# Two 3x3 convolutions with group norms: the order of the rows of the transformed input

## The chip, the cores and the metric

The kernel runs on one core of a Trainium2 chip, as one launch. The metric is the device time of an execution in microseconds; a median over several executions stands for a kernel. TensorE multiplies matrices and accumulates in PSUM; VectorE, ScalarE and GpSimd work element by element on SBUF and PSUM; SyncE issues most DMAs. In the profile they are PE (and PEld for its weight loads), DVE, ACT, POOL and SP.

## What is computed

A residual block on x of 2 images, 512 channels, 64 x 64 pixels, in bf16:

```python
h = conv3(_silu(gn(x, g1, be1)), w1)
emb = _silu(t_emb) @ w_emb
h = h + emb.reshape(B, C, 1, 1)
h = conv3(_silu(gn(h, g2, be2)), w2)
return x + h
```

`gn` normalizes each of four groups of 128 channels over its channels and all pixels, `conv3` is a 3x3 convolution with padding 1 from 512 to 512 channels.

## The kernel before, in words

**Tiling.** Channels lie in four blocks of 128 (`ct` of the input, `ot` of the output), one block on the 128 partitions. An image is cut into two chunks of 32 rows, so there are four chunks in each of the two layers. One chunk and one `ot` make a "set" (`one_set`, L789); 32 sets follow each other.

**Transform.** The convolution is done in a transformed form. Rows go in groups of four output rows (`TH`), eight groups to a chunk (`TR`). For each group six rows of input are combined into six "positions" 0 to 5; for each position the kernel columns `kx` = 0, 1, 2 are three taps, read with an offset of one element each. A chunk of a `ct` has a tile V (eight tiles `Vbuf`, four per chunk, in turn; so a tile is written again for the chunk after next). In it a position takes NI = 8 x 66 = 528 elements, its "slot". The weights are transformed in the same way into tiles U. TensorE multiplies U by V into one of three PSUM buffers `acc` and ScalarE and VectorE combine the positions into output rows y.

**Two kinds of chunk.** In the first chunk of layer 0 all six positions are stored and multiplied (`col` false in `is_col`, L561). In all others positions 0 and 5 are transformed along the columns too and lie behind the four slots of positions 1 to 4, from element 4 NI on; there slots 0 to 3 hold positions 1, 2, 3, 4. In the first chunk slot i holds position i. The last two chunks of layer 1 replace the products of positions 1 and 3 by another form (`v_more`, `v_more_split`, `rhs_more_split`, L540 to L559).

**Who writes V.** `make_v` (L584) is VectorE's work for a block, with some operations on ScalarE (`scaled`). Positions come in pairs: with `pr` and `qs`, two terms each, from vt, one operation writes positions 1 and 3 as their sums (L601) and one writes 2 and 4 as their differences (L602). In the first chunk a third writes 0 and 5 from the activated input `a_tmp` (L604) and a fourth adds `rs` (a src tile) to both (L605). The destination of each is one access with two blocks of 528 elements; `vv` (L593) gives it for the first two.

**Who reads V.** `row_pair` (L671) makes the matmuls of a pair of positions, 3 taps x 4 `ct` each, through `rhs_row` (L564); `col_pair` (L681) reads the parts behind 4 NI. A set uses the pairs (1, 3), then for a `col` chunk columns (1, 2), then (2, 4), then (0, 5) or columns (0, 3).

**Order.** Every operation is first a node with an estimated cost in a planner (`_Plan`, L25). Its dependencies are exact masks of elements (`region`, L62), and the planner lists the operations of each engine in its own order, mixing sets, chunks and the weights' transform (`u_blocks`, L485, which needs transposes on TensorE, L386, and copies on ScalarE, L510). All VectorE operations of a kind have one line (L317 for two tensors, L322 and L330 for others), all main matmuls have L660, and ScalarE's have L347. The planner only orders: the waits (semaphores) between and within engines are put in afterwards by the framework, from what each instruction reads and writes.

Of the kernel before, what the change touches and what calls it, by code (L numbers as in the profile page):

```python
# [187 lines left out]
def kernel(  # L188
# [24 lines left out]
    TR = 8  # L213
# [13 lines left out]
    WARM = (11, 12)  # L227
    DVE_SUMS = (1,)
    COL0 = (1, 2, 3)
    POS_ORDER = (1, 3, 2, 4, 0, 5)  # L230
    assert C % P == 0 and E % P == 0 and C // 4 == P and H % CR == 0 and NFREE == 512

    x_v = x.rearrange("b (ct p) h w -> b ct p (h w)", p=P)
# [304 lines left out]
    more_buf = lambda ct: (a_tmp + src)[ct]  # L538

    def v_more(V, X):  # L540
        rows = lambda kx, st: view(V, kx, [[2 * NI, 2], [WP, TR], [st, W // st]])
        dst = lambda o, n: view(X, o, [[n * TR, 2], [n, TR], [1, n]])
        tt(dst(0, W), rows(0, 1), rows(2, 1), ALU.subtract)
        tt(dst(4 * NC, W // 2), rows(1, 2), rows(2, 2), ALU.add)
        tt(dst(6 * NC, W // 2), rows(2, 2), rows(1, 2), ALU.subtract)
# [3 lines left out]
    def v_more_split(V, at, D):  # L549
        rows = lambda kx, st: view(at, kx, [[NI, 2], [WP, TR], [st, W // st]])  # L550
        tt(view(D, 0, [[W * TR, 2], [W, TR], [1, W]]), rows(0, 1), rows(2, 1), ALU.subtract)
        dst = lambda i: view(V, i * 2 * NI, [[NC, 2], [W // 2, TR], [1, W // 2]])
        tt(dst(0), rows(1, 2), rows(2, 2), ALU.add)
        tt(dst(1), rows(2, 2), rows(1, 2), ALU.subtract)

    def rhs_more_split(V, D, j, c):
        if c in (0, 3):
            return view(D, j * 2 * NC + (1 if c == 3 else 0), [[W, TR], [2, W // 2]])
        return view(V, (c - 1) * 2 * NI + j * NC, [[1, NC]])  # L559

    def is_col(layer, b, ch):  # L561
        return layer == 1 or b * NCH + ch in COL0

    def rhs_row(V, pos, kx, col):  # L564
        i = pos - 1 if col else pos
        return view(V, i * NI + kx, [[WP, TR], [1, W]])

    def rhs_col(V, j, c, o=4 * NI):
        if c in (0, 3):
# [14 lines left out]
    def make_v(V, at, rs, col, on_act, split=False):  # L584
        n2 = 2 * NI
        q2 = view(vt, 0, [[2 * WP, TR], [1, 2 * WP]])
        s2 = view(vt, n2, [[2 * WP, TR], [1, 2 * WP]])
        s_, r_ = (view(vt, n2 + i * WP, [[2 * WP, TR], [1, WP]]) for i in range(2))
        qs, pr = (view(vt, i * WP, [[n2, 2], [2 * WP, TR], [1, WP]]) for i in range(2))
        rows2 = lambda j: view(at, j * WP, [[TH * WP, TR], [1, 2 * WP]])  # L590
        pair = lambda j, d: view(at, j * WP, [[d * WP, 2], [TH * WP, TR], [1, WP]])
        flat = lambda t, i: view(t, i * NI, [[WP, TR], [1, WP]])
        vv = lambda i: view(V, (i if col else i + 1) * NI, [[n2, 2], [WP, TR], [1, WP]])  # L593
        scaled(q2, rows2(1), 4.0, on_act[0])
        tt(s2, rows2(3), rows2(1), ALU.subtract)
        tt(q2, q2, rows2(3), ALU.subtract)
        scaled(flat(rs, 0), r_, 0.25, on_act[1])
        scaled(flat(rs, 1), s_, -4.0, on_act[1])
        scaled(s_, s_, 2.0, on_act[2])
        if not split:  # L600
            tt(vv(0), pr, qs, ALU.add)  # L601
        tt(vv(1), pr, qs, ALU.subtract)  # L602
        if not col:
            tt(view(V, 0, [[5 * NI, 2], [WP, TR], [1, WP]]), pair(0, 5), pair(2, 1), ALU.subtract)  # L604
            tt(view(V, 0, [[5 * NI, 2], [1, NI]]), view(V, 0, [[5 * NI, 2], [1, NI]]),  # L605
               view(rs, 0, [[NI, 2], [1, NI]]), ALU.add)
            return
        vt_, vo = (rs, n2) if split else (vt, 0)
        tt(view(vt_, vo, [[NI, 2], [WP, TR], [1, WP]]), pair(0, 5), pair(2, 1), ALU.subtract)
        if split:  # L610
            tt(view(at, 0, [[NI, 2], [WP, TR], [1, WP]]), pr, qs, ALU.add)
        w05f = view(vt_, vo, [[1, n2]])
        tt(w05f, w05f, view(rs, 0, [[1, n2]]), ALU.add)
        o = 4 * NI
        tt(view(V, o, [[W, 2 * TR], [1, W]]), view(vt_, vo, [[WP, 2 * TR], [1, W]]),
           view(vt_, vo + 2, [[WP, 2 * TR], [1, W]]), ALU.subtract)
        odd = view(vt_, vo + 1, [[WP, 2 * TR], [2, W // 2]])
        evn = view(vt_, vo + 2, [[WP, 2 * TR], [2, W // 2]])
        tt(view(V, o + 4 * NC, [[W // 2, 2 * TR], [1, W // 2]]), odd, evn, ALU.add)
        tt(view(V, o + 6 * NC, [[W // 2, 2 * TR], [1, W // 2]]), evn, odd, ALU.subtract)  # L620
# [47 lines left out]
        count["acc"] += 1  # L668
        return acc[(count["acc"] - 1) % 3]

    def row_pair(pair, U, V, col, gid, split):  # L671
        a = next_acc()
        todo = []
        for i, pos in enumerate(pair):
            for ct in range(CT):
                taps = [(u_tap(U[ct], pos, kx), rhs_row(V[ct], pos, kx, col)) for kx in range(NKX)]
                todo.append((i, a[:, i], [t[0] for t in taps], [t[1] for t in taps], 0.218 * NKX))
        groups(todo, a, (gid, pair))
        return a
# [60 lines left out]
    def final_set(U, V):  # L740
        b, ch = chunks[-1]
        ot = CT - 1
        y = next_y()
        dma(y[:], x_v[b, ot][:, ch * CR * W:(ch + 1) * CR * W], writes=[y[:]])
        y4 = y[:].rearrange("p (t f w) -> p f t w", f=TH, w=W)
        gid = "final"
        more_pair(U, gid)
        a = col_pair((1, 2), U, V, gid, 10.0)
        act(mb[:].rearrange("p k j n -> p j k n"), a, scale=0.5)
        tt(sd[:, 0], mb[:, 0], mb[:, 1], ALU.add)  # L750
        tt(sd[:, 1], mb[:, 0], mb[:, 1], ALU.subtract)
        n = CR * W // 2
        y12, y03 = y4[:, 1:3], y4[:, 0:TH:TH - 1]
        both = lambda t, o: view(t, o, [[0, 2], [W, TR], [1, W]])
        tt(y12, y12, both(m1, 0), ALU.add)
        tt(y03, y03, both(m1, 0), ALU.add)
        for i in range(2):
            sd4 = sd[:, i].rearrange("p j (t w) -> p j t w", t=TR)
            tt(sd4, sd4, view(y, i, [[(TH - 1) * W, 2], [TH * W, TR], [2, W // 2]]), ALU.add)
        z = view(stage[1], 0, [[NFREE, 2], [1, NFREE]])  # L760
        e = view(stage[2], 0, [[NFREE, 2], [1, NFREE]])
        a = row_pair((4,), U, V, True, gid, 1)
        act(w_[:, 1, 1], a[:, 0], scale=KAPPA)
        tt(e[:, 0], m1[:, 1], w_[:, 1, 1], ALU.add)
        tt(w_[:, 0, 1], m1[:, 1], w_[:, 1, 1], ALU.subtract)
        act(z[:, 0], w_[:, 0, 1], scale=2.0)
        act(z[:, 1], e[:, 0], scale=4.0)
        ts(e[:, 1], w_[:, 0, 1], 8.0)
        tt(y12, y12, t4(z), ALU.add)
        a = row_pair((2,), U, V, True, gid, 1)  # L770
        q = [view(vt, i * NFREE, [[1, NFREE]]) for i in range(3)]
        act(q[1], a[:, 0], scale=KAPPA)
        act(q[0], a[:, 0], scale=-KAPPA)
        act(q[2], a[:, 0], scale=-KAPPA)
        pm = lambda i: view(vt, i * NFREE, [[NFREE, 2], [1, NFREE]])
        tt(e, e, pm(1), ALU.add)
        tt(y12, y12, t4(pm(0)), ALU.add)
        aa = col_pair((0, 3), U, V, gid)
        for h in range(2):
            for k, op in ((0, ALU.add), (1, ALU.subtract)):  # L780
                part = lambda t: t.rearrange("p j (t w) -> p j t w", t=TR)[:, :, h * TR // 2:(h + 1) * TR // 2]
                tt(view(y, k + h * n, [[(TH - 1) * W, 2], [TH * W, TR // 2], [2, W // 2]]), part(sd[:, k]),
                   part(aa[:, :, k]), op)
            o = view(y, h * n, [[(TH - 1) * W, 2], [TH * W, TR // 2], [1, W]])
            tt(o, o, e[:, :, h * NFREE // 2:(h + 1) * NFREE // 2].rearrange("p j (t w) -> p j t w", w=W), ALU.add)
            dma(out_v[b, ot][:, ch * CR * W + h * n:ch * CR * W + (h + 1) * n], y[:, h * n:(h + 1) * n],
                reads=[y[:, h * n:(h + 1) * n]], eng=("ACT", "SP")[h], due=clock["t"] + 10)

    def one_set(layer, idx, ot, U, V):  # L789
# [12 lines left out]
        def first_pair():  # L802
            if more:
                (more_cols(U, V, gid) if idx == len(chunks) - 2 else more_pair(U, gid))
            else:
                a = row_pair((1, 3), U, V, col, gid, 1)
                if layer == 0:
                    act(m1[:], a[:], func=ACT.Identity, scale=KAPPA, accum=acc_sum(0))
                else:
                    act(m1[:], a[:], scale=KAPPA)  # L810
# [3 lines left out]
        if col:  # L814
            ab = col_pair((1, 2), U, V, gid)
            act(mb[:].rearrange("p k j n -> p j k n"), ab, scale=0.5)
        a = row_pair((2, 4), U, V, col, gid, 1)
        act(w_[:, 1], a[:], scale=KAPPA)
        if late:
            first_pair()  # L820
# [14 lines left out]
        tt(w_[:, :, 0], w_[:, :, 0], w_[:, :, 1], ALU.add)  # L835
        w03 = t4(w_[:, :, 0])
        if not col:
            a = row_pair((0, 5), U, V, col, gid, 1)
            m05 = view(sd, 0, [[NFREE, 2], [1, NFREE]])
            act(m05, a[:], func=ACT.Identity, accum=acc_sum(3))  # L840
            tt(y4[:, 0:TH:TH - 1], t4(m05), w03, ALU.add)
# [246 lines left out]
```

## Time and profile before

| | |
|---|---|
| median of 3 runs | 496.41 us (496.39 to 496.76) |
| the profiled execution | 495.44 us |
| its span, first to last instruction | 493.5 us |
| granted TensorE clock | 0.998 |
| ScalarE busy | 391.9 us (79%) |
| GpSimd busy | 44.0 us (9%) |
| moved by DMA | 55.54 MB, 113 GB/s in the mean |

A row of the timeline gives the start (us from the first instruction), the duration, engine, line, operation, the tiles it writes and reads, shapes and how many were merged into the row; in brackets stands the idle time of the engine before it and what released it. A row of the view of waits reads: who waited, for whom, total us, how often, the longest. A group of the view by shapes has the count, busy us, mean ns of one, and the idle time before.

### The profile page before, as it was taken

The numbers are of one execution on the slowest core, as the hardware profiler recorded it, in microseconds if no ns is written. First come the engines' busy times: TensorE is split into PE (matmuls) and PEld (weight loads), VectorE is DVE, ScalarE is ACT, GpSimd is POOL, SyncE is SP. The second block draws the span as 40 slices with busy tenths as digits, with TensorE's granted clock in tenths as the row PEclk, the third lists the DMA queues.
The fourth block names the chain that finished last, engine by engine and source line by source line (L and its number), as shares of the span: only waits on it lengthen the run. The fifth ranks groups of instructions, "written<-read, shape, count | busy, mean of one in ns | idle before, by whom it ended". The sixth has DMA issues, their size and how long they took to land.

```text
span 493.5 us, 8648 instructions
## 1 busy us (share of the span) xinstructions
PE 480.2 (97%) x3241; PEld 290.1 (59%) x3241; DVE 462.2 (94%) x1003; ACT 391.9 (79%) x536; POOL 44.0 (9%) x106
## 2 busy tenths in 40 slices
PE   8889999999999999999999999999999999999994
PEld 7755544465555655456655565555555667668572
DVE  2889999999999999999999999999999999997596
ACT  1598999999999859999999999687577685534452
POOL 2210000042020040000000001200000000000010
PEclk9999999999999999999999999999999999999999
DMA  8533211760121333215425212445553643334345
GB/s 305 186 97 98 89 63 46 273 257 0 48 83 44 109 83 127 86 57 165 154 65 166 88 44 53 129 121 130 130 130 85 174 121 95 87 63 109 83 109 151
DMA packets 17316, 55.54 MB, mean 113 GB/s; under 512 B 1915, under 2 KB 3067, under 8 KB 16507
## 3 DMA queue, kind: packets, MB, share of 16 engines
q1 hardware_dynamic: 14912, 46.86, 27.8%
q0 software_dynamic: 2160, 7.87, 9.7%
q8 instruction: 25, 0.41, 0.3%
q10 hardware_dynamic: 203, 0.27, 0.1%
q14 instruction: 16, 0.13, 0.1%
HBM read 38.22 MB, written 16.78 MB: 111 GB/s over the span
## 4 chain that ended last, share of the span: by engine, by line
PE 44%; DVE 15%; ACT 3%; issue 2%; DVEq 0%
PE acc L660 42%; DVE V L317 3%; DVE y L317 3%; DVE vt L317 2%; DVE w L317 2%; ACT a_tmp L347 1%; PE xa L386 1%; DVE y L330 1%; DVE sd L317 1%; DVE U L317 1%; DVE stage L317 0%; PE xb L386 0%; ACT mb L347 0%; DVE src L317 0%; ACT vt L347 0%
## 5 line engine op out<-in xcount | busy, mean ns | idle before, releaser
L660 PE MATMUL acc<-V,U 128*128 128x512 bf16 (+1 forms) x2400 | 434.7, 338 | 3.5 <-DVE V L317 3.4
L660 PEld LDWEIGHTS <-U 128*128 128x128 bf16 x2592 | 249.7, 98 | 180.2 <-issue 4.9
L317 DVE TENSOR_TENSOR V<-vt 128x1056 bf16<-128x1056 bf16 (+2 forms) x132 | 89.8, 692 | 0.9 <-ACT vt L347 0.2
L347 ACT ACTIVATE w<-acc 128x1024 bf16<-128x1024 f32 (+1 forms) x32 | 32.3, 1010 | 23.0 <-PE acc L660 14.2
L347 ACT ACTIVATE a_tmp<-src,arena 128x2112 bf16<-128x2112 bf16 x20 | 42.9, 2145 | 5.7 <-DVE stage L317 4.0
L317 DVE TENSOR_TENSOR w<-m,w 128x1024 bf16<-128x1024 bf16 (+1 forms) x63 | 42.8, 680 | 4.8 <-ACT w L347 4.7
L347 ACT ACTIVATE mb<-acc 128x1024 bf16<-128x1024 f32 x32 | 32.6, 1017 | 16.3 <-PE acc L660 16.1
L317 DVE TENSOR_TENSOR U<-U 128x768 bf16<-128x768 bf16 (+2 forms) x96 | 44.3, 485 | 0.4 <-ACT U L510 0.2
L347 ACT ACTIVATE m<-w 128x512 bf16<-128x512 bf16 x62 | 37.2, 625 | 6.9 <-DVE w L317 6.9
L347 ACT ACTIVATE src<-vt 128x528 bf16<-128x528 bf16 x54 | 33.8, 640 | 8.0 <-DVE vt L317 8.0
L317 DVE TENSOR_TENSOR vt<-a_tmp 128x1056 bf16<-128x1056 bf16 x56 | 38.8, 701 | 0.4
L510 ACT COPY U<-xa 128x768 bf16<-128x768 bf16 x31 | 24.9, 803 | 9.8 <-PE xa L386 9.7
L386 PEld LDWEIGHTS <-stage 128*128 128x128 bf16 x288 | 26.2, 143 | 9.4
L347 ACT ACTIVATE y<-y 128x2048 bf16<-128x2048 bf16 x16 | 30.4, 1900 | 0.0
L347 ACT ACTIVATE m<-acc 128x1024 bf16<-128x1024 f32 x24 | 24.4, 1018 | 5.2 <-DVE y L317 3.2
L347 ACT ACTIVATE a_tmp<-V,arena 128x2112 bf16<-128x2112 bf16 x12 | 25.8, 2153 | 2.8 <-DVE arena L330 2.8
L317 DVE TENSOR_TENSOR sd<-mb 128x512 bf16<-128x512 bf16 x64 | 26.0, 417 | 1.5 <-ACT mb L347 1.5
L579 POOL MEMSET a_tmp<- 128x64 bf16 x32 | 5.7, 178 | 239.8 <-DVE vt L317 209.1
L365 POOL DMA_DIRECT2D y<-in_x_dram x15 | 13.2, 882 | 136.3 <-DVE y L317 134.8
L317 DVE TENSOR_TENSOR y<-sd,acc 128x512 bf16<-128x512 bf16 (+1 forms) x34 | 22.0, 686 | 2.1 <-PE acc L660 1.9
L317 DVE TENSOR_TENSOR y<-m,w 128x1024 bf16<-128x1024 bf16 x31 | 21.3, 686 | 2.4 <-ACT m L347 1.8
L347 ACT ACTIVATE src<-V 128x2048 bf16<-128x2048 bf16 x12 | 22.9, 1905 | 0.1
(118 smaller groups left out, 504.1 us busy)
## 6 DMA issues: line engine op xcount, KB each, us to landing
stage<-in_w_dram SPq DMA_DIRECT2D x32, 288.0 KB, 2.8
src<-h_scr SPq DMA_DIRECT2D x16, 528.0 KB, 3.9
h_scr<-y SPq DMA_DIRECT2D x16, 512.0 KB, 3.0
y<-in_x_dram POOLq DMA_DIRECT2D x15, 512.0 KB, 5.6
out_dram<-y SPq DMA_DIRECT2D x15, 512.0 KB, 2.6
V<-in_x_dram SPq DMA_DIRECT2D x6, 1024.0 KB, 5.1
src<-in_x_dram SPq DMA_DIRECT2D x4, 528.0 KB, 3.8
V<-in_x_dram SPq DMA_DIRECT2D x4, 512.0 KB, 6.8
```

What stands on the lines that cost most here:

```text
L317: lambda: nc.vector.tensor_tensor(out=out, in0=in0, in1=in1, op=op), [in0, in1], [out], **kw)
L330: nc.vector.scalar_tensor_tensor(out=out, in0=in0, scalar=scalar, in1=in1, op0=op0, op1=op1, **extra)
L347: nc.scalar.activation(out=out, in_=in_, func=fn, scale=scale, **extra)
L365: q.dma_start(out=out, in_=in_, **extra)
L386: nc.tensor.transpose(sel(t), in_, ident[:in_.shape[0], :in_.shape[0]])
L510: lambda: nc.scalar.copy(out=out, in_=sel(bank.get())), [tok], [out])
L579: pool(lambda r=r: nc.gpsimd.memset(rows[:, r, 1:W + 1], 0.0), [], [rows[:, r, 1:W + 1]], cost=0.2)
L660: nc.tensor.matmul(ap, lhsT=l, rhs=r, start=k == 0, stop=k == total[key] - 1)
```

## The change

The six positions get a new order in V: 1, 3, 2, 4, 0, 5 (`SLOT`; `POS_ORDER`, which it replaces, was used nowhere). In a chunk with four stored positions the order is 1, 3, 2, 4. So the two blocks of each pair write lie side by side, and an access of two blocks of 528 becomes one run of 1,056 elements. `rhs_row` looks the slot up. The special forms of the last chunks read positions 1 and 3 from slots 0 and 1 instead of 0 and 2.

```diff
-    POS_ORDER = (1, 3, 2, 4, 0, 5)
+    SLOT = (1, 3, 2, 4, 0, 5)
...
     def v_more(V, X):
-        rows = lambda kx, st: view(V, kx, [[2 * NI, 2], [WP, TR], [st, W // st]])
+        rows = lambda kx, st: view(V, kx, [[NI, 2], [WP, TR], [st, W // st]])
...
-        dst = lambda i: view(V, i * 2 * NI, [[NC, 2], [W // 2, TR], [1, W // 2]])
+        dst = lambda i: view(V, i * NI, [[NC, 2], [W // 2, TR], [1, W // 2]])
...
-        return view(V, (c - 1) * 2 * NI + j * NC, [[1, NC]])
+        return view(V, (c - 1) * NI + j * NC, [[1, NC]])
...
-    def rhs_row(V, pos, kx, col):
-        i = pos - 1 if col else pos
-        return view(V, i * NI + kx, [[WP, TR], [1, W]])
+    def rhs_row(V, pos, kx):
+        return view(V, SLOT.index(pos) * NI + kx, [[WP, TR], [1, W]])
...
-        vv = lambda i: view(V, (i if col else i + 1) * NI, [[n2, 2], [WP, TR], [1, WP]])
+        vv = lambda i: view(V, 2 * i * NI, [[NI, 2], [WP, TR], [1, WP]])
...
         if not col:
-            tt(view(V, 0, [[5 * NI, 2], [WP, TR], [1, WP]]), pair(0, 5), pair(2, 1), ALU.subtract)
-            tt(view(V, 0, [[5 * NI, 2], [1, NI]]), view(V, 0, [[5 * NI, 2], [1, NI]]),
-               view(rs, 0, [[NI, 2], [1, NI]]), ALU.add)
+            w05 = view(V, 4 * NI, [[1, n2]])
+            tt(view(V, 4 * NI, [[NI, 2], [WP, TR], [1, WP]]), pair(0, 5), pair(2, 1), ALU.subtract)
+            tt(w05, w05, view(rs, 0, [[1, n2]]), ALU.add)
             return
...
-    def row_pair(pair, U, V, col, gid, split):
+    def row_pair(pair, U, V, gid):
...
-                taps = [(u_tap(U[ct], pos, kx), rhs_row(V[ct], pos, kx, col)) for kx in range(NKX)]
+                taps = [(u_tap(U[ct], pos, kx), rhs_row(V[ct], pos, kx)) for kx in range(NKX)]
```

The calls of `row_pair` lose two arguments, and the file one line, so lines behind L564 move up by one. In the built programs every engine has the same instructions in the same order. What differs beside the accesses is which instructions carry a wait; on ScalarE, GpSimd and SyncE these are the same. On TensorE six matmuls lose their wait, seven get one, and one weight load loses one of two. The six are, by their start in the trace of before, the matmuls of 24.38, 31.96, 35.47, 207.43, 267.02 and 383.69 us. On VectorE the waits for TensorE of the V writes at 22.94, 31.20 and 42.92 us are gone, and that at 36.32 us waits for VectorE alone; 26 V writes lose a wait for VectorE itself, and seven other instructions get one. The waits at 22.09 and 37.08 us on TensorE stay, but for an earlier VectorE instruction.

More of the change, by code (lines that the diff above doesn't have):

```diff
@@ L761, in final_set @@
         e = view(stage[2], 0, [[NFREE, 2], [1, NFREE]])
-        a = row_pair((4,), U, V, True, gid, 1)
+        a = row_pair((4,), U, V, gid)
         act(w_[:, 1, 1], a[:, 0], scale=KAPPA)
@@ L769, in final_set @@
         tt(y12, y12, t4(z), ALU.add)
-        a = row_pair((2,), U, V, True, gid, 1)
+        a = row_pair((2,), U, V, gid)
         q = [view(vt, i * NFREE, [[1, NFREE]]) for i in range(3)]
@@ L805, in first_pair @@
             else:
-                a = row_pair((1, 3), U, V, col, gid, 1)
+                a = row_pair((1, 3), U, V, gid)
                 if layer == 0:
@@ L816, in one_set @@
             act(mb[:].rearrange("p k j n -> p j k n"), ab, scale=0.5)
-        a = row_pair((2, 4), U, V, col, gid, 1)
+        a = row_pair((2, 4), U, V, gid)
         act(w_[:, 1], a[:], scale=KAPPA)
@@ L837, in one_set @@
         if not col:
-            a = row_pair((0, 5), U, V, col, gid, 1)
+            a = row_pair((0, 5), U, V, gid)
             m05 = view(sd, 0, [[NFREE, 2], [1, NFREE]])
```

## The prediction

> **What bounds the kernel now.** I read the page first, then the waits by engine, then the stretches, and last the timeline of TensorE and VectorE around every place where TensorE waited.
>
> ```profile
> span 493.5 us, 8648 instructions
> PE 480.2 (97%) x3241; PEld 290.1 (59%) x3241; DVE 462.2 (94%) x1003; ACT 391.9 (79%) x536; POOL 44.0 (9%) x106
> ```
>
> TensorE is busy for 97% of the span, VectorE for 94%. So the time can only fall by what TensorE loses to waits, plus the head and the tail. The view of TensorE's waits, longest first, shows how little that is:
>
> ```profile
> PE acc L660 <- DVE V L317: 3.4, 5, 1.2
> PE acc L966 <- DMA V<-in_x_dram: 1.1, 2, 0.7
> PE acc L941 <- DVE ones_bf L911: 1.1, 1, 1.1
> PE acc L402 <- DVE acc L330: 0.7, 1, 0.7
> ```
>
> The main matmuls (L660) wait for one thing alone: VectorE's writes of V, five times, 3.4 us. The other three lines belong to the first 20 us, which the change does not touch. The stretches say where those five lie (columns: from and to; busy of PE, weight loads, DVE, ACT, POOL; granted clock; DMA share; GB/s):
>
> ```profile
> 22.09:40.00 17.91, 16.46 (x138) 10.26 (x138) 16.19 (x46) 15.02 (x23) 3.14 (x7) 1.00 0.31 83
> 40.00:207.00 167.00, 166.88 (x974) 89.98 (x973) 164.61 (x366) 155.34 (x219) 18.80 (x37) 1.00 0.30 100
> 207.00:384.00 177.00, 176.24 (x1097) 102.60 (x1097) 175.03 (x374) 153.52 (x207) 9.25 (x20) 1.00 0.38 108
> 384.00:480.00 96.00, 96.00 (x691) 66.78 (x689) 85.11 (x152) 55.94 (x76) 7.21 (x10) 1.00 0.43 106
> ```
>
> TensorE loses time in the first chunk and a little between 207 and 384; after 384 it runs without a gap to the tail. VectorE has 2.4 us of idle time in the second row and 2.0 us in the third, so it is nearly as full, and a gain on TensorE lasts only if VectorE moves too. These are the places (start, listed duration, then the idle time and its releaser):
>
> ```profile
> 20.53 0.38 PE L386 MATMUL xb<-ident,stage 128*128 128x128 bf16 x3
> 22.09 0.81 PE L660 MATMUL acc<-V,U 128*128 128x512 bf16 x3 [1.18 <-DVE V L317]
> 22.74 0.51 PE L386 MATMUL xa<-ident,stage 128*128 128x128 bf16 x6
> 26.87 0.28 PE L402 MATMUL acc<-arena,ones_neg 128*128 128x2 f32 x2
> 27.18 0.83 PE L660 MATMUL acc<-V,U 128*128 128x512 bf16 x3
> 31.00 0.34 PE L386 MATMUL xb<-ident,stage 128*128 128x128 bf16 x3
> 31.96 0.81 PE L660 MATMUL acc<-V,U 128*128 128x512 bf16 x3 [0.62 <-DVE V L317]
> 35.47 0.82 PE L660 MATMUL acc<-V,U 128*128 128x512 bf16 x3
> 37.08 1.47 PE L660 MATMUL acc<-V,U 128*128 128x512 bf16 x6 [0.80 <-DVE V L317]
> ```
>
> Listed ends are modelled: the three matmuls of 22.09 are listed with 0.81 us, yet the next instruction starts 0.65 us later, so 0.16 us of each group's listed time overlaps the next. What a stall costs is therefore its idle time plus some 0.16 us: 1.35 us at 22.09 (the transposes of 20.53 would let it start at 20.73), 0.79 us at 31.96, 0.96 us at 37.08 (0.65 behind 35.47 is 36.12). At 27.18 up to 0.31 us (the step from 26.87) is lost behind two small matmuls, too short to be printed as idle.
>
> **The change part by part.** No instruction is added or removed and the order on every engine stays, so only two things can change: what an instruction lasts, and what it waits for.
>
> *Durations.* The pair writes now cover one run. Rows by shape:
>
> ```profile
> L317 DVE TENSOR_TENSOR V<-vt 128x1056 bf16<-128x1056 bf16 x60 | 42.2, 703 | 0.9 <-ACT vt L347 0.2
> L317 DVE TENSOR_TENSOR vt<-a_tmp 128x1056 bf16<-128x1056 bf16 x56 | 38.8, 701 | 0.4
> ```
>
> A pair write in two runs lasts 703 ns; an equally long operation that fills a single run of vt lasts 701. I take the same duration: 60 x 2 ns = 0.1 us for all, at most. Matmuls read the same number of rows of the same width from another slot: nothing.
>
> *Waits.* In the built program of before, the waits fit a tracker that takes an access as one range from its first to its last element. The write of positions 1 and 3 (slots 1 and 3) then covers slot 2 as well, that of 2 and 4 covers slot 3, and the pair 0 and 5 covers the whole tile. So instructions that share no element wait for each other. With the pairs side by side these waits are gone from the built program. There are three kinds.
>
> (a) VectorE waits for TensorE. VectorE's rows in the first chunk:
>
> ```profile
> 19.84 0.70 DVE L317 TENSOR_TENSOR V<-vt 128x1056 bf16<-128x1056 bf16 x1
> 20.58 0.71 DVE L317 TENSOR_TENSOR V<-a_tmp 128x1056 bf16<-128x1056 bf16 x1
> 21.32 0.71 DVE L317 TENSOR_TENSOR V<-vt 128x1056 bf16<-128x1056 bf16 x1
> 21.95 0.21 DVE L330 SCALAR_TENSOR_TENSOR arena<-arena 128x1 f32<-128x1 f32 x1
> 22.35 0.14 DVE L324 TENSOR_SCALAR arena<-arena 128x1 f32<-128x1 f32 x1
> 22.94 0.71 DVE L317 TENSOR_TENSOR V<-V,src 128x1056 bf16<-128x1056 bf16 x1 [0.44 <-PE acc L660]
> 26.78 0.35 DVE L317 TENSOR_TENSOR U<-U,g1t 128x384 bf16<-128x384 bf16 x1
> 34.44 0.71 DVE L317 TENSOR_TENSOR V<-vt 128x1056 bf16<-128x1056 bf16 x1
> 36.32 0.71 DVE L317 TENSOR_TENSOR V<-V,src 128x1056 bf16<-128x1056 bf16 x1 [1.17 <-PE acc L660]
> ```
>
> The write at 22.94 adds to slots 0 and 5 and waits for the matmuls of 22.09, which read position 3; without that wait it follows 22.35 at once (0.07 us is the usual step behind an operation of 0.14): 0.52 us. At 36.32 the same costs 1.17 idle plus 0.08 of overlap, 1.25 us.
>
> (b) VectorE waits for itself. 19.84 to 20.58 and 20.58 to 21.32 are steps of 0.74 us; the operation of 21.32, of the same length, is followed without a wait after 0.63. A wait on the operation directly in front costs 0.11 to 0.12 us. Two stand ahead of 22.94 (0.24 us), two more ahead of 36.32, and one between the two halves of nearly every later block, such as
>
> ```profile
> 158.37 1.45 DVE L317 TENSOR_TENSOR V<-vt 128x1056 bf16<-128x1056 bf16 x2
> ```
>
> where two writes take 1.45 instead of 0.63 + 0.70 = 1.33. The Trainium skill, VectorE: DVE Perf Modes, section "The DRAIN you can't avoid", speaks against this part: it says that a chain of copies takes as long with a semaphore after each as with one at the end. This trace disagrees, by 0.74 against 0.63 us. By that rule part (b) would be worth nothing; what this would leave is the first rival below.
>
> (c) TensorE waits for VectorE. The matmuls of 22.09 read position 3 (slot 3) and wait for the write that starts at 21.32, which holds 2 and 4; without this they need the one that ends at 20.54. Those of 31.96 and 37.08 read position 2 and wait for the add to 0 and 5 (37.08 is 0.05 after 36.32 + 0.71). Three more lie at the ends of chunks, where VectorE already writes positions 1 and 3 of the chunk after next into a tile whose position 2 is still read:
>
> ```profile
> 206.66 0.71 DVE L317 TENSOR_TENSOR V<-vt 128x1056 bf16<-128x1056 bf16 x1
> 207.43 1.91 PE L660 MATMUL acc<-V,U 128*128 128x512 bf16 x8 [0.55 <-DVE V L317]
> 266.27 0.70 DVE L317 TENSOR_TENSOR V<-vt 128x1056 bf16<-128x1056 bf16 x1
> 266.30 1.32 PE L660 MATMUL acc<-V,U 128*128 128x256 bf16 x6
> 383.69 0.38 PE L660 MATMUL acc<-V,U 128*128 128x512 bf16 x1 [0.21 <-DVE V L317]
> ```
>
> Each matmul starts 0.05 us behind the end of such a write. The price is 0.55 + 0.16 = 0.71 at 207.43 and 0.21 + 0.16 = 0.37 at 383.69. Of the six at 266.30, four are half as wide as 512 columns; at 0.65 / 3 = 0.22 and half of it, the last would start 0.66 behind the first and be listed as ending 0.38 later, at 267.34; it ends at 267.62: 0.28 us.
>
> *The sum, place by place.* At 22.09 TensorE gains 1.35. At 27.18 it meets a true wait, for the weights that VectorE finishes at 26.78 + 0.35. VectorE is 0.24 + 0.52 = 0.76 us earlier by then, so these come at 26.37 and TensorE keeps 0.76 of its 1.35: the stall moves there. At 31.96 the 0.79 goes (its true predecessors on VectorE, the write of positions 2 and 4 and a block of weights, are done by then): 1.55. At 37.08 the 0.96 goes: 2.51. VectorE itself is then ahead by 0.76 + 0.11 + 0.11 + 1.25 = 2.23, and by what ScalarE's earlier start adds. ScalarE has room, because it waits for the two others here:
>
> ```profile
> 33.17 0.80 ACT L510 COPY U<-xa 128x768 bf16<-128x768 bf16 x1 [0.86 <-PE xa L386]
> 37.68 1.18 ACT L347 ACTIVATE src<-vt 128x528 bf16<-128x528 bf16 x2 [0.60 <-DVE vt L317]
> ```
>
> The loads of weights follow TensorE's transposes and land in 2.8 us, in three buffers, so they move with it:
>
> ```profile
> stage<-in_w_dram SPq DMA_DIRECT2D x32, 288.0 KB, 2.8
> ```
>
> So all three engines enter the second stretch 2.5 us early. Then 0.71, 0.28 and 0.37 are added: 2.51 + 1.36 = 3.87 us. VectorE has to keep up with the 0.71: in the stretch before 207 it loses some six self-waits of 0.12, 0.7 us. The tail behind the last matmul keeps its length. Ends: if every stall in which L660 waits for V went in full (1.35 + 0.31 + 0.79 + 0.96 + 1.36) it would be 4.8 us; if only the 0.76 and the late 1.36 lasted, 2.1 us. I take 3.8, next to the sum, because each step above has its true predecessor early enough.
>
> The profiled execution took 495.44 us, its span 493.5 and 1.9 around it; the sum gives 491.6 for it. The median of the three runs is 496.41, 1.0 above the profiled one, and I carry the difference over: 492.6 us.
>
> **The rivals.**
>
> First, the self-waits are free, as that page has it. Then VectorE is 0.52 ahead at 26.78, TensorE 2.27 at 37.08, and VectorE, without the 0.7, can hold TensorE back by up to half a microsecond before 384. Gain about 3.3, time 493.1. The two step lengths speak against it; for it, that a few steps of 0.11 are thin ground.
>
> Second, the gain is handed back, because other true waits bind in the first chunk as the weights do at 27.18 (VectorE and ScalarE also make the weights there). Then 0.76 + 1.36 = 2.1: 494.3. For it: VectorE was idle for only 1.7 us between 22.09 and 40. Against it: most of that idle time is waits of kind (a).
>
> Third, the waits that went were covered by others that stay, and nothing moves: 496.4. Against it: TensorE's starts follow the ends of exactly those writes within 0.05 us.
>
> Fourth, slower: a write in one run takes VectorE longer than in two. About 50 of the 60 fall between 40 and 384, where VectorE has 4.4 us idle. It decides from (3.8 + 4.4) / 50 = 0.16 us more for each, 865 ns instead of 703. At the rate of
>
> ```profile
> L317 DVE TENSOR_TENSOR y<-sd,acc 128x512 bf16<-128x512 bf16 x30 | 20.4, 720 | 2.1 <-PE acc L660 1.9
> ```
>
> (1.4 ns an element, twice the normal) each would take 1,480 ns, 39 us more in all, and 39 - 8 = 31 us would come out behind: about 527 us. The 701 ns of vt, a single run already, speaks against it.
>
> **How the numbers follow.** Forecast 0.68, first rival 0.13, second 0.10, third 0.05, fourth 0.04. Time 492.6 us. The range goes from 491.6 (all 4.8 us) to 494.6, which takes in the first two rivals. 0.2%, 1.0 us, is about what a measurement of this kernel can tell from no change: faster by more is the forecast and the first two rivals, 0.91; the same 0.05; slower 0.04.
>
> **What would show it.** Right: no idle time of VectorE for L660 at the writes of V; the first main matmul at 20.7; a stall for weights near 26.4; no wait of L660 for V left, so that the wait line of 3.4 us shrinks below 1; the matmul of 37.08 at 34.6, of 207.43 near 204.2, of 383.69 near 379.8; pair writes at 703 ns. Wrong: the pair of writes still at 1.45 us (first rival); TensorE's idle time between 22 and 40 not below 1 us (second); pair writes above 0.75 us (fourth).

## The result, and the profile after

The kernel after takes 492.24 us (median of 6 runs, 491.98 to 493.62), beside 496.43 us for the kernel before (6 runs): a ratio of 0.9921, 95% interval 0.9907 to 0.9935, so between 3.2 and 4.6 us less. The prediction was 492.6 us, in a range of 491.6 to 494.6. Its profiled execution took 493.62 us, its span 491.7; that is the longest of the six, and what made it long comes below.

Lines behind the cut helper have numbers one lower than before (L660 is now L659). The view of TensorE's waits of the kernel after, longest first (columns: total, times, longest):

```profile
PE acc L965 <- DMA V<-in_x_dram: 1.6, 3, 0.9
PE acc L940 <- DVE ones_bf L910: 1.1, 1, 1.1
PE acc L402 <- DVE acc L330: 1.0, 2, 0.7
PE acc L659 <- DVE U L317: 0.6, 1, 0.6
```

The line of 3.4 us, L660 for V, is gone altogether; a wait for weights (U) of 0.6 us has come. The stretches of the same profile (from and to; PE, weight loads, DVE, ACT, POOL; granted clock; DMA share; GB/s):

```profile
10.00:15.00 5.00, 4.13 (x60) 3.87 (x60) 2.93 (x15) 1.44 (x2) 1.02 (x2) 0.77 0.98 395
15.00:20.00 5.00, 4.28 (x92) 4.19 (x91) 3.51 (x17) 1.99 (x2) 1.20 (x2) 0.89 0.54 187
40.00:207.00 167.00, 167.00 (x975) 90.07 (x974) 164.03 (x366) 155.27 (x218) 20.08 (x37) 1.00 0.29 100
207.00:384.00 177.00, 177.00 (x1105) 103.20 (x1103) 175.44 (x376) 153.42 (x208) 9.24 (x20) 1.00 0.39 110
```

Between 40 and 384 us TensorE now has no gap. The first two rows are not the change's doing: the granted clock stood at 0.77 and 0.89 between 10 and 20 us, and the first write of V came at 21.09 us instead of 19.84. The profile of before has 1.00 in both stretches:

```profile
10.00:15.00 5.00, 4.30 (x86) 4.05 (x86) 3.21 (x18) 1.62 (x2) 1.02 (x2) 1.00 0.99 404
15.00:20.00 5.00, 4.28 (x89) 4.19 (x87) 4.52 (x21) 2.75 (x4) 1.20 (x2) 1.00 0.53 178
```

So has the third profile of the kernel after, in the table below. Start times of the two executions can therefore be compared only from that write on. The main matmuls of the first chunk in the timeline of TensorE:

```profile
21.98 0.82 PE L659 MATMUL acc<-V,U 128*128 128x512 bf16 x3
...
27.23 0.38 PE L402 MATMUL acc<-arena,ones_neg 128*128 128x2 f32 x2 [0.29 <-DVE acc L330]
28.20 0.83 PE L659 MATMUL acc<-V,U 128*128 128x512 bf16 x3 [0.58 <-DVE U L317]
...
32.18 0.82 PE L659 MATMUL acc<-V,U 128*128 128x512 bf16 x3
```

and of VectorE (idle time and its releaser in brackets):

```profile
21.09 0.70 DVE L317 TENSOR_TENSOR V<-vt 128x1056 bf16<-128x1056 bf16 x1
21.71 0.70 DVE L317 TENSOR_TENSOR V<-a_tmp 128x1056 bf16<-128x1056 bf16 x1
22.32 0.70 DVE L317 TENSOR_TENSOR V<-vt 128x1056 bf16<-128x1056 bf16 x1
...
23.41 0.70 DVE L317 TENSOR_TENSOR V<-V,src 128x1056 bf16<-128x1056 bf16 x1
24.02 0.70 DVE L317 TENSOR_TENSOR vt<-a_tmp 128x1056 bf16<-128x1056 bf16 x1
24.64 0.35 DVE L317 TENSOR_TENSOR U<-U 128x384 bf16<-128x384 bf16 x1
24.91 0.43 DVE L322 TENSOR_SCALAR vt<-a_tmp 128x1056 bf16<-128x1056 bf16 x1
25.25 0.35 DVE L317 TENSOR_TENSOR U<-U,g1t 128x384 bf16<-128x384 bf16 x1
25.52 0.15 DVE L322 TENSOR_SCALAR arena<-acc 128x1 f32<-128x1 f32 x1
25.59 0.70 DVE L317 TENSOR_TENSOR vt<-vt,a_tmp 128x1056 bf16<-128x1056 bf16 x1
26.75 0.16 DVE L317 TENSOR_TENSOR arena<-arena,gb 128x1 f32<-128x1 f32 x1 [0.46 <-POOL arena L438]
...
27.79 0.35 DVE L317 TENSOR_TENSOR U<-U,g1t 128x384 bf16<-128x384 bf16 x1
```

The writes of V follow each other in steps of 0.62 us (0.74 before), the add of 23.41 waits for nobody, and the first main matmul starts 0.90 us behind the first write (2.24 before). Then something new: at 26.21 (25.59 + 0.62) VectorE runs dry until 26.75, for GpSimd. The weights of 27.79 come that much later, and TensorE stands at 28.20 until they are there.

The table sets start times against the first write of V, for every profile taken in this study. All are starts from the traces, less that of the write (a difference of two printed rows can be 0.01 off); the heads name a place by its time in the first profile of before. "End" is the end of the last matmul.

| kernel | first write of V | 22.09 | 27.18 | 37.08 | 207.43 | 267.02 | 383.69 | end |
|---|---|---|---|---|---|---|---|---|
| before | 19.84 | 2.24 | 7.34 | 17.24 | 187.58 | 247.18 | 363.85 | 466.84 |
| before, second | 19.44 | 2.24 | 7.34 | 17.24 | 187.57 | 247.17 | 363.85 | 466.83 |
| before, third | 20.33 | 2.24 | 7.34 | 17.24 | 188.39 | 247.99 | 364.68 | 467.67 |
| after | 21.09 | 0.90 | 7.11 | 15.26 | 185.16 | 244.47 | 360.77 | 463.77 |
| after, second (again) | 20.09 | 2.22 | 7.22 | 15.45 | 185.39 | 244.71 | 361.01 | 464.00 |
| after, third | 19.35 | 0.89 | 7.11 | 15.26 | 184.90 | 244.22 | 360.52 | 463.51 |
| first_only | 20.52 | 0.90 | 7.11 | 15.27 | 186.43 | 246.03 | 362.72 | 465.71 |
| cols_only | 21.24 | 2.24 | 7.34 | 17.23 | 187.08 | 246.39 | 362.69 | 465.69 |
| pair05 | 20.31 | 1.99 | 7.16 | 15.65 | 186.03 | 245.62 | 362.27 | 465.26 |
| selfwait | 22.48 | 0.89 | 7.11 | 15.27 | 185.75 | 245.25 | 361.55 | 464.55 |
| gap | 19.89 | 0.89 | 7.11 | 15.27 | 184.91 | 244.23 | 360.53 | 463.52 |
| eps_dve | 20.65 | 0.90 | 6.56 | 14.71 | 184.35 | 243.67 | 359.97 | 462.96 |
| eps_dve, second (eps_again) | 20.87 | 0.89 | 6.55 | 14.71 | 184.35 | 243.67 | 359.97 | 462.96 |

Two things are to be read from it. Behind the first write two profiles of one kernel agree within 0.02 us, or differ by a fixed step, but for the second of after, which comes below; the head, ahead of it, runs from 19.35 to 22.48 us with no order by kernel. And the time of each profiled execution is first write + end + 8.75 us (before: 19.84 + 466.84 + 8.76 = 495.44; after: 21.09 + 463.77 + 8.76 = 493.62), so the tail is the same everywhere, within 0.02 us. The end column is the change, without the chance of the head. The second profile of after stands out by its 2.22: its clock dip came later, over the first main matmuls, and these are its two stretches:

```profile
15.00:20.00 5.00, 4.28 (x82) 4.19 (x80) 4.49 (x22) 2.54 (x3) 1.20 (x2) 0.90 0.55 197
20.00:25.00 5.00, 5.00 (x79) 4.54 (x77) 4.76 (x15) 4.64 (x6) 2.49 (x3) 0.76 0.30 75
```

At 27.18 only 0.11 us of that delay of 1.32 us is left (7.22 against 7.11): the stall for weights took up the rest.

### The profile page after: what moved, and what is told of

Same layout as the page of the kernel before. It is cut to its first block, busy times and chain, and to the rows that moved or that the text cites. A ratio compares the mean times of both kernels' runs of the same rounds, so it can differ in the third digit from the quotient of the medians.

```text
span 491.7 us, 8645 instructions
## 1 busy us (share of the span) xinstructions
PE 480.6 (98%) x3241; PEld 290.9 (59%) x3241; DVE 460.5 (94%) x1003; ACT 391.3 (80%) x536; POOL 47.3 (10%) x106
## 4 chain that ended last, share of the span: by engine, by line
PE 92%; DVE 4%; DMA 2%; POOL 1%; issue 0%; SPq 0%; ACT 0%; DVEq 0%
PE acc L659 87%; PE xa L386 2%; DMA V<-in_x_dram 2%; DVE y L317 1%; PE xb L386 1%; PE acc L965 1%; DVE sd L317 1%; DVE V L317 1%; POOL arena L435 0%; SPq L365 0%; DVE vt L317 0%; PE acc L967 0%; DVE m L317 0%; DVE w L317 0%; ACT mb L347 0%
## 5 line engine op out<-in xcount | busy, mean ns | idle before, releaser
L659 PE MATMUL acc<-V,U 128*128 128x512 bf16 (+1 forms) x2400 | 434.3, 338 | 0.6 <-DVE U L317 0.6
L659 PEld LDWEIGHTS <-U 128*128 128x128 bf16 x2592 | 249.7, 98 | 176.6 <-DVE U L317 0.9
```

Source lines behind the costliest of these rows:

```text
L659: nc.tensor.matmul(ap, lhsT=l, rhs=r, start=k == 0, stop=k == total[key] - 1)
```

## The experiments

The kernels `first_only`, `cols_only`, `pair05` and `selfwait` take two slot orders, one for the first chunk (FIRST) and one for the others (COLS), through one helper; the instructions and their order stay those of before and after:

```
 def rhs_row(V, pos, kx, gid):
     order = FIRST if gid == (0, 0, gid[2]) else COLS
     return view(V, order.index(pos) * NI + kx, [[WP, TR], [1, W]])
```

**The change once more.** The kernel after, unaltered, on the chip of the next three.

> The changed kernel once more, for a profile whose first 20 us are undisturbed (in the first profile of it the granted clock fell to 0.77 between 10 and 15 us and everything behind began about 1.2 us late). My theory: 492.2 us (491.9 to 492.6); with the clock at 1.00 in the first 20 us the first main matmul starts at 20.7, the stall for weights stands near 26.4 with 0.5 to 0.7 us of idle time, the matmul of 37.08 starts at 34.6, that of 207.43 near 204.2 and that of 383.69 near 379.8; span 489.6. Rival, that part of the gain is another one than the waits of the prediction: the span is below 489 with the same starts up to 384, or these starts come earlier.

492.48 us (492.30 to 492.84) beside 496.52 for before, ratio 0.9909 [0.9888, 0.9931]. The gain is there again, 4.0 us. The clock of its profile dipped once more, so the start times expected of an undisturbed head have to be looked for in the third profile; its span, 490.9 us, is above the 489.6 expected.

**The first chunk alone.**

```
-    SLOT = (1, 3, 2, 4, 0, 5)
+    FIRST = (1, 3, 2, 4, 0, 5)
+    COLS = (1, 2, 3, 4)
```

> New order in the first chunk alone; the other chunks keep 1, 2, 3, 4. My theory: only the 2.51 us of the first chunk, 493.9 us (493.6 to 494.2) against 496.4; the stalls of L660 for V stay at the three chunk ends, 0.5, 0 and 0.2 us idle. Rival, that the first chunk hands its gain back and only the 0.76 us of the early VectorE work last: 495.6.

494.40 us, ratio 0.9947 [0.9928, 0.9967]: by the interval 492.9 to 494.9 us, which holds the 493.9 expected and leaves out the rival's 495.6; the median itself lies 0.2 us above the range on record. The table says more: 17.24 - 15.27 = 1.97 us are gained by 37.08, not the 2.51 forecast. The end shows still less, 466.84 - 465.71 = 1.13, and the line of TensorE's waits says that three waits for V are left:

```profile
PE acc L670 <- DVE V L318: 1.2, 3, 0.5
```

Two of them are those of 207.43 and 383.69; the third, of 0.46 us at 159.42, isn't in the first profile of before. It is in the third, which is shown below, and against that one the end gains 467.67 - 465.71 = 1.96 us.

**The later chunks alone.**

```
+    FIRST = (0, 1, 2, 3, 4, 5)
+    COLS = (1, 3, 2, 4)
```

> New order in all chunks but the first. My theory: the three late stalls go, 0.71 + 0.28 + 0.37 = 1.36 us, 495.0 us (494.8 to 495.3) against 496.4; the first chunk stalls as before (1.18, 0.62 and 0.80 us idle). Rival, that the waits of VectorE for itself cost time of their own beside the stalls (some 15 later ones of 0.12): down to 493.5. Rival, that TensorE's late stalls come back at another place: 496.

494.74 us, ratio 0.9966 [0.9950, 0.9983], a gain of 1.8 us (1.36 expected); as an interval of the time that is 494.0 to 495.7, which leaves out the 493.5 and the 496 of the rivals. The first chunk stands as before to 0.01 us, and its three waits are the only ones left:

```profile
PE acc L670 <- DVE V L318: 2.6, 3, 1.2
```

The late stalls are gone without any help from the first chunk. The sum of both gains, 2.1 + 1.8 = 3.9 us, is that of the whole (4.0). The end column says the same without the chance of the head: against the third profile of before, which shares a delay with these two and with the first profile of after (shown below), the parts gain 1.96 and 467.67 - 465.69 = 1.98 us, and the whole 467.67 - 463.77 = 3.90. So the two parts are independent.

**The pair 0 and 5 alone.** In the first chunk only 0 and 5 lie side by side; 1 and 3, and 2 and 4, still interleave.

```
+    FIRST = (1, 2, 3, 4, 0, 5)
+    COLS = (1, 2, 3, 4)
```

> Only the pair 0 and 5 put side by side, in the first chunk (order 1, 2, 3, 4, 0, 5); pairs 1, 3 and 2, 4 cross as before, and the later chunks are as before. My theory: the add to 0 and 5 no longer waits for matmuls and the matmuls of 31.96 and 37.08 no longer wait for it; the first matmul still waits for the write of 2 and 4 and starts at 21.8, but what that loses is mostly hidden by the weights' stall: 2.25 us gain, 494.2 us (493.8 to 494.5). Rival, that the three kinds of pair share the gain of the first chunk in proportion to the stalls that they cause at first sight (1.35 us of it at 22.09): about 1.5 us, 494.9 or more.

494.64 us, ratio 0.9960 [0.9940, 0.9979], which as a time (493.5 to 495.5) leaves both numbers open. The trace doesn't: by 37.08 it has 17.24 - 15.65 = 1.59 us, so the 2.25 expected was too much, and the rival's 1.5 is near. As a share it is 1.59 of the 1.97 us that all three pairs yield there, more than the rival gave it (1.5 of 2.51): the add that covered the whole tile was the dearest of the three. This kernel also prices the self-waits by themselves, because the writes of V no longer touch the one directly in front, while the first main matmul keeps its false wait for the third write (timelines of VectorE and of TensorE):

```profile
20.31 0.70 DVE L318 TENSOR_TENSOR V<-vt 128x1056 bf16<-128x1056 bf16 x1
20.93 0.70 DVE L318 TENSOR_TENSOR V<-a_tmp 128x1056 bf16<-128x1056 bf16 x1
21.55 0.70 DVE L318 TENSOR_TENSOR V<-vt 128x1056 bf16<-128x1056 bf16 x1
```

```profile
22.30 0.81 PE L670 MATMUL acc<-V,U 128*128 128x512 bf16 x3 [0.93 <-DVE V L318]
```

Two steps of 0.62 instead of 0.74, and the matmul behind them 2.24 - 1.99 = 0.25 us earlier: a wait on the operation in front costs 0.12 us, and in the first chunk it reaches TensorE. That is the first rival's point, and it falls there.

**Where the rest of the first chunk's gain went.** GpSimd has two tiny operations between the statistics and the weights. Its timeline before:

```profile
22.58 0.22 POOL L435 TENSOR_SCALAR arena<-arena 128x1 f32<-128x1 f32 x1 [1.08 <-DVE arena L324]
22.89 0.57 POOL L438 TENSOR_TENSOR arena<-arena,neg_half 128x1 f32<-128x1 f32 x1
```

and after:

```profile
23.58 2.11 POOL L435 TENSOR_SCALAR arena<-arena 128x1 f32<-128x1 f32 x1 [0.95 <-DVE arena L324]
25.77 0.95 POOL L438 TENSOR_TENSOR arena<-arena,neg_half 128x1 f32<-128x1 f32 x1
```

The same single-element operation takes 0.22 us before and 2.11 after. Before, VectorE stood still at that moment (its wait of 0.44 us ahead of 22.94, the one that the change removes); after, VectorE goes from operation to operation (its rows of 23.41 to 25.25, above), and L435 ends at 25.69, just behind VectorE's operation of 25.52. That one is the first in this stretch that reads PSUM instead of SBUF, and also the only one on a single element; no run here tells which of the two lets GpSimd in. The Trainium skill, SBUF — State Buffer, section "Who interferes with whom", says that a VectorE instruction with two inputs in SBUF contends with a GpSimd instruction that reads SBUF, and that one with at most one such input, outside the two-port modes, doesn't. These rows agree with it if the operation of 24.91, with one input in SBUF, ran in a two-port mode, which no row shows. To test whether VectorE's order decides, VectorE's operation of 25.52 was issued three places earlier:

```
+        dve = [i for i in order if nodes[i].eng == "DVE"]
+        order.remove(dve[52])
+        order.insert(order.index(dve[49]), dve[52])
         for i in order:
             nodes[i].emit()
```

> The kernel after, with one VectorE operation on a single element, which reads its input from PSUM (L322, arena<-acc, 25.52 us), issued three operations earlier, in front of U<-U at 24.64. Theory: GpSimd's L435, listed from 23.58 to 25.69 us, is locked out by VectorE's operations with two inputs in SBUF that follow each other without a gap, and gets in at the first one that reads only PSUM. Then L435 ends at about 24.9 us instead of 25.69 (1.3 us listed instead of 2.1); GpSimd's second operation (L438) then waits in the same way for the next gap, at 26.2 us, so VectorE's wait for it stays at 0.4 to 0.6 us and the time at 492.3 us (491.9 to 492.9). Rival: L435 is slow for a reason of its own on GpSimd; it stays at 2.1 us and ends at 25.7.

492.34 us, ratio 0.9919 [0.9905, 0.9933]. The timelines of GpSimd and of VectorE in it:

```profile
22.38 1.23 POOL L438 TENSOR_SCALAR arena<-arena 128x1 f32<-128x1 f32 x1 [0.95 <-DVE arena L327]
23.69 1.83 POOL L441 TENSOR_TENSOR arena<-arena,neg_half 128x1 f32<-128x1 f32 x1
```

```profile
23.44 0.15 DVE L325 TENSOR_SCALAR arena<-acc 128x1 f32<-128x1 f32 x1
...
25.55 0.16 DVE L320 TENSOR_TENSOR arena<-arena,gb 128x1 f32<-128x1 f32 x1 [0.46 <-POOL arena L441]
```

The first operation (here L438) shrinks from 2.11 to 1.23 us and ends at 23.61, right behind the operation that was moved; now the second one is held, 1.83 us instead of 0.95, until VectorE runs dry (it ends at 25.52, and less the 0.57 that it takes alone that is 24.95; VectorE's operation of 24.39 ends its step of 0.62 at 25.01). VectorE's wait stays at 0.46 and the time doesn't move, as expected. What GpSimd waits for lies in VectorE's work (that one operation, or an idle VectorE), not in anything of its own.

**One operation less on GpSimd.** The added constant goes into the VectorE operation in front, in every place where that one is on VectorE; the clamp of the variance at zero is left out.

```
-            ts(nvar[:], nvar[:], 0.0, op=ALU.min, c2=-1.0, op1=ALU.mult)
+            ts(rstd[:], nvar[:], -1.0, op=ALU.mult, c2=EPS, op1=ALU.add)
...
-        pool(lambda: nc.gpsimd.tensor_scalar(out=rstd[:], in0=nvar[:], scalar1=EPS, scalar2=None, op0=ALU.add),
-             [nvar[:]], [rstd[:]])
+        def eps():
+            if not quick:
+                nc.gpsimd.tensor_scalar(out=rstd[:], in0=nvar[:], scalar1=EPS, scalar2=None, op0=ALU.add)
+        pool(eps, [rstd[:]] if quick else [nvar[:]], [rstd[:]])
```

> The kernel after, with the addition of the small constant to the variance (L435 on GpSimd) folded into the VectorE operation in front of it (L324) wherever that one is on VectorE; the clamp at zero, which that operation held, is left out, and GpSimd keeps only the power (L438). Theory: with one GpSimd operation instead of two only one has to get in between VectorE's; the power runs at 25.5 to 26.1 us (0.57), in time for VectorE at 26.2, so VectorE's wait of 0.46 us for GpSimd goes, the weights come 0.5 us earlier and TensorE's stall at 28.20 shrinks from 0.58 to about 0.1; all that follows is 0.5 us earlier: 491.8 us (491.5 to 492.2). Rival 1: GpSimd is not locked out; the power runs at once, at 23.6 to 24.2: same time, but listed there. Rival 2: the gain in the first chunk is taken back by a later true wait, and the time stays at 492.3 to 492.5.

492.47 us, ratio 0.9915 [0.9902, 0.9929]. GpSimd's power is held for 2.44 us and is still in time, at 25.57; VectorE takes its result without a wait at 25.77. Its row, and then TensorE's:

```profile
23.13 2.44 POOL L440 TENSOR_TENSOR arena<-arena,neg_half 128x1 f32<-128x1 f32 x1 [0.94 <-DVE arena L324]
```

```profile
26.35 0.28 PE L402 MATMUL acc<-arena,ones_neg 128*128 128x2 f32 x2
27.21 0.83 PE L661 MATMUL acc<-V,U 128*128 128x512 bf16 x3 [0.58 <-DVE U L317]
```

The matmul that waits for the weights starts 7.11 - 6.56 = 0.55 us earlier, which is the stretch that GpSimd cost. (The text on record expected the printed idle of 0.58 to shrink to 0.1. It didn't, since L402 in front, which also hung on GpSimd, moved up as well.) The 0.55 lasts to the end column, 463.51 - 462.96 against the third profile of after; against the first it is 0.81. But the median is that of after, above the 491.5 to 492.2 expected and where the second rival had it. The kernel was therefore run again, beside the kernel after on one chip.

> The kernel with the constant added on VectorE, again, beside the kernel after on the same chip. Theory: its part behind the first write of V is 0.8 us shorter than in the kernel after (462.96 against 463.77 us to the last matmul), and its median of 492.47 came from a later first write (20.65 us in the profile). Then its lowest times lie 0.8 us under those of the kernel after, near 491.2, and its median between 491.3 and 492.5. Rival: the later first write belongs to this kernel, and the median is 492.4 to 492.6 again.

> The kernel after, a third profile, beside the one with the constant on VectorE. Behind its first write of V: 0.90 us to the first main matmul, 463.8 to the last, unless the granted clock falls below 1 behind that write. Time 472.5 us plus the time of the first write, 492.3 us (491.9 to 492.9).

492.56 us (491.23 to 494.40) beside 492.82 (491.62 to 494.92); ratios to before 0.9909 [0.9882, 0.9935] and 0.9927 [0.9902, 0.9952]. The order is the expected one, but the lowest times lie 0.4 us apart and not 0.8, the difference of 0.3 us between the medians is far inside the intervals, and 492.56 lies in the rival's range (492.4 to 492.6) and just above that of the theory. The third profile of after, 491.62 us, ended at 463.51 behind its first write, not at 463.8, because the delay at 137 us shown below was absent. The gain of the kernel with the constant on VectorE is in the trace, 0.55 to 0.81 us at the end of the last matmul. Its first write stood at 20.65 and 20.87 us in its two profiles; whether that belongs to this kernel, as the rival has it, or is chance, two profiles don't settle. It isn't shown to beat the kernel after.

**The self-waits of the later chunks.**

```
+    FIRST = (1, 3, 2, 4, 0, 5)
+    COLS = (2, 1, 3, 4)
```

> The new order in the first chunk, and the order 2, 1, 3, 4 in all later ones: the pairs 1 and 3 lie side by side, 2 and 4 span the whole tile, so the second pair write waits for the first again (14 more waits of VectorE on itself than in the kernel after), while no matmul waits for a write that it doesn't read. Theory: TensorE leads and VectorE has room, so the steps of 1.45 us for two writes come back (1.33 in the kernel after) and the time stays that of the kernel after, 492.3 us (492.0 to 492.7). Rival, as the prediction had it: the 0.7 us of self-waits in front of 207 holds TensorE back there, and the time is 0.3 to 0.7 longer, 492.8 to 493.0.

493.14 us (491.92 to 495.79), ratio 0.9927 [0.9913, 0.9941]: above the theory's range (492.0 to 492.7) and near the rival's number, but not by its cause, and the theory was badly built. In this order the write of 2 and 4 covers the slots of 1 and 3, so it brings back not only VectorE's self-waits but also a false wait of the matmuls that read 1 and 3, which the expectation denied. It stands at 161.38 in TensorE's timeline, right behind the pair of writes of 159.88 (1.45 us, the self-wait included):

```profile
161.38 0.81 PE L670 MATMUL acc<-V,U 128*128 128x512 bf16 x3 [0.46 <-DVE V L318]
```

Its price, 0.46 + 0.16 = 0.62 us, is most of the 0.78 by which the end column is longer than in the first profile of after. Behind it, matched matmul by matmul, 0.14 us is made up again, and three steps of 0.08 to 0.10 us follow (at 197.30, 220.62 and 233.47 in the profile of after), too short to be printed as idle. What the self-waits of the later chunks cost by themselves was not separated; beside the 0.12 us within the pair of writes of 159.88, at most these 0.28 us are left for them.

**What varies in the kernel before.** Its first profile took 495.44 us, 1.0 below the median of the runs; two more were taken.

> The kernel before, unchanged, for a second profile of it. Its first profile took 495.44 us, 1.0 below the median of its runs, and had its first write of V at 19.84 us. If the missing 1 us lies ahead of the transformed input, this profile has that first write at 20.1 to 21.2 us and the same distances behind it: 2.24 us to the first main matmul, 187.6 to the one that stood at 207.43, 466.8 to the last matmul. If it lies in the waits of the first chunk, the distances themselves are 0.5 to 1 us longer. Time 496.4 us (495.4 to 496.8).

> The kernel before, a third profile. In two profiles of it all distances behind the first write of V agree within 0.01 us, and that write stood at 19.84 and 19.44 us, while half of its executions take over 496.4 us. If all of the spread lies ahead of that write (x's landing and the clock), this profile too has 2.24 us to the first main matmul and 466.8 to the last one, and its time is 475.6 us plus the time of the first write: 495.0 to 498.

The second, 495.02 us, repeats the first to 0.01 us behind a first write that came earlier, not later as the text on record had it. The third, 496.75 us, does not: its end is at 467.67 instead of 466.84, and the expectation that all the spread lies in the head is refuted. TensorE's waits in it count a sixth time:

```profile
PE acc L660 <- DVE V L317: 3.8, 6, 1.2
```

The chain in its timelines (GpSimd, VectorE, TensorE):

```profile
137.70 2.43 POOL L435 TENSOR_SCALAR arena<-arena 128x1 f32<-128x1 f32 x1 [1.39 <-DVE arena L324]
```

```profile
140.82 0.16 DVE L317 TENSOR_TENSOR arena<-arena,gb 128x1 f32<-128x1 f32 x1 [0.76 <-POOL arena L438]
...
159.65 1.45 DVE L317 TENSOR_TENSOR V<-vt 128x1056 bf16<-128x1056 bf16 x2
```

```profile
161.16 1.03 PE L660 MATMUL acc<-V,U 128*128 128x512 bf16 x4 [0.46 <-DVE V L317]
```

In the first profile the same L435 took 0.60 us:

```profile
137.20 0.60 POOL L435 TENSOR_SCALAR arena<-arena 128x1 f32<-128x1 f32 x1 [1.39 <-DVE arena L324]
```

So in some executions GpSimd gets in between two VectorE operations at this place, and in others it is held for 2.43 us. Where it is held, VectorE is 0.8 us late from there on, and 20 us later the second of a pair of writes (positions 2 and 4, ending at 161.10) delays a matmul at 161.16 that waits for it only because its range spans position 3. The kernel after meets the same hold in its own profile:

```profile
136.52 2.43 POOL L435 TENSOR_SCALAR arena<-arena 128x1 f32<-128x1 f32 x1 [1.44 <-DVE arena L324]
```

and loses 0.26 us by it at the end (463.77 against 463.51), not 0.84, since the matmul has no such wait any more. Its third profile is the one without the hold:

```profile
134.78 0.60 POOL L435 TENSOR_SCALAR arena<-arena 128x1 f32<-128x1 f32 x1 [1.45 <-DVE arena L324]
```

Six of the eleven profiles that have this operation show the hold: the third of before, the first two of after, `first_only`, `cols_only` and `selfwait`. With the constant on VectorE, GpSimd's power is held in its place, 2.78 us in the first profile and 0.96 in the second, and both end at 462.96.

## Why the prediction was right, step by step

**Durations.** The 60 pair writes last 704 ns in one run, 703 before. The fourth rival, a slower write, is out:

```profile
L317 DVE TENSOR_TENSOR V<-vt 128x1056 bf16<-128x1056 bf16 x60 | 41.2, 704 | 0.3
```

**Waits of VectorE for TensorE and for itself.** From the first write to the add of slots 0 and 5 it was 22.94 - 19.84 = 3.10 us and is 23.41 - 21.09 = 2.32: 0.78, for 0.24 + 0.52 = 0.76 predicted. The pair of writes that took 1.45 us takes 1.33, the number predicted, in this row of the timeline after:

```profile
158.35 1.33 DVE L317 TENSOR_TENSOR V<-vt 128x1056 bf16<-128x1056 bf16 x2
```

**Waits of TensorE.** At 22.09 it gained 2.24 - 0.90 = 1.34 (1.35 predicted). Between 27.18 and 37.08 it gained another 1.98 - 0.23 = 1.75 (0.79 + 0.96 = 1.75 predicted). The late three are read between executions with the same luck at 137 us, since both orders then carry the same delay: from 37.08 to 207.43, 267.02 and 383.69 the first profile of before against the third of after gives 0.70, 0.28 and 0.37 (0.71, 0.28, 0.37 predicted).

**The term that was mis-sized** is the 0.76 us that TensorE was to keep of its 1.35 at 27.18. It kept 0.23. The prediction had the weights follow VectorE, 0.76 us earlier; it did not look at GpSimd's operation between them, which used the idle time that the change takes away. VectorE came 5.29 - 4.50 = 0.79 us earlier to its operation ahead of it (25.13 before, 25.59 after, each less the first write) and then waited for GpSimd. So the first chunk yielded 1.98 instead of 2.51 us. This is a little of the second rival, another true wait in the first chunk, but on GpSimd rather than on the weights' makers that it named, and it took 0.53 us, not 1.75. Moving GpSimd's addition away brought 0.55 us back in the trace, so the cause is shown. The start times named as signs of being right, 34.6, 204.2 and 379.8, stand in the third profile of after almost to the digit (34.62, 204.25, 379.87), but by luck: its first write came 0.49 us earlier than in the profile that the prediction used, and that hides the 0.53.

**The sum.** 1.98 + 1.35 = 3.33 us, where 3.8 was forecast; the end column has the same, 466.84 - 463.51. That it is also the 3.3 of the first rival is chance, since the self-waits do cost their 0.12 us. The median moved by 4.2 (4.0 and 3.8 on the two other chips where it was measured beside before), and not all executions of before are like its profile. With GpSimd held at 137 us in both, the end moves by 467.67 - 463.77 = 3.90 us: the sixth false wait, which the profile behind the prediction did not contain, adds 0.6. The forecast carried the 1.0 us between that profile and the median over unchanged; where an execution has the hold, part of it is a cost that the change also removes. How many of the timed executions have it is not on record, so its share in the median is argued and not shown. Two errors of about half a microsecond, one each way, lie behind a forecast that missed by 0.4; that it came so near is partly luck. The 0.3 us between 3.90 and 4.2 is within the interval; the head's spread can hold it, and nothing shows more.

**The third rival**, that nothing moves, is excluded by the ratio.

## What to carry to other kernels

Where dependencies are tracked as one range from first to last element, the order of rows in a buffer decides who waits for whom: put together what one instruction writes, and keep out of its range what others still read. Before a wait is counted as pure gain, look for who uses the idle time that it leaves, above all an engine that needs a gap in another's work. And a single profile shows one of several courses of an execution: take a second and a third before the difference between profile and median is carried over as a constant.

## What the runs showed of the hardware

A single-element GpSimd operation on SBUF (L435) takes 0.22 us where VectorE stands still, and up to 2.4 us where VectorE runs operations with SBUF inputs one behind the other; whether it slips in varies from execution to execution, 0.60 or 2.43 us at the same place in the same kernel. The granted clock of TensorE dropped somewhere between 10 and 25 us in four of the thirteen profiles (after, again, cols_only, selfwait). Over a stretch of 5 us it reads 0.57 to 0.78; in stretches of half a microsecond it is 0.50 for some 3.4 us, in selfwait for twice as long, and 1.00 on both sides. In three of them the first write of V came at 21.09 us or later, and the latest, 22.48 us, had the lowest clock:

```profile
10.00:15.00 5.00, 4.43 (x65) 4.24 (x62) 1.81 (x11) 0.80 (x1) 1.02 (x2) 0.57 1.00 412
```

The fourth, again, with its dip at 19 to 22.4 us, lost 1.3 us at the first main matmul and kept 0.2 of it to the end (464.00 against 463.77). The seven timed executions of before whose mean clock was 0.988 or 0.989 took 498.0 to 499.3 us, beside medians of 496.5 and 496.6, so a lower clock is a part of what spreads the times. What sets off the dip is not known from these runs.
